# Transposing normalised rows by DMA instead of on TensorE, in two attention fronts

## The chip, the cores and the metric

One core of a Trainium2 chip runs the whole program. The metric is the time of one execution in device microseconds (us); lower is better. TensorE multiplies matrices (PE in the profile, PEld for its weight loads), VectorE is DVE, ScalarE is ACT, GpSimd is POOL, and SyncE (SP) issues nearly all DMAs, one after the other, from one queue.

## The reference

The input `A_x` has 2048 tokens of 512 features in bf16. Four layers are applied with residuals: attention, long convolution, attention, long convolution, each on layer-normalised rows.

```python
def _A_ref(x, wqkv, wo):             # H = 32 heads of Dh = 16, W = 8 keys, dilation 2
    qkv = (x @ wqkv).reshape(B, S, 3, H, Dh).transpose(2, 0, 3, 1, 4)
    q, k, v = qkv[0], qkv[1], qkv[2]
    idx = pos[:, None] - 2 * arange(8)[None, :]; mask = idx >= 0
    kg, vg = k[:, :, idx], v[:, :, idx]          # idx clipped at 0
    logits = einsum("bhsd,bhswd->bhsw", q, kg) * Dh ** -0.5
    attn = softmax(where(mask, logits, -1e9), axis=-1)
    return einsum("bhsw,bhswd->bhsd", attn, vg) -> (B, S, D) @ wo
def _B_ref(u, A, B, C, log_dt, Dskip):
    K = real(einsum("dn,dnl,dn->dl", C, exp(dt * A * l), dt * B))   # 2048 taps per feature
    return irfft(rfft(u) * rfft(K)) [first 2048] + u * Dskip
x = x + _A_ref(layernorm(x), A_wqkv, A_wo)
x = x + _B_ref(layernorm(x), ...)
x = x + _A_ref(layernorm(x), A_wqkv, A_wo)
x = x + _B_ref(layernorm(x), ...)
```

## The kernel before

**Tokens.** Token 16p + a lies on partition p in slot a (a = 0..15). A block b is four slots, that is 512 tokens; there are four blocks. `x_blk` and `xn` hold the normalised rows of one block, 128 partitions x (4 slots x 512 features).

**A front** is what each attention layer does before its core: normalise the rows of a block, turn them so that features lie on the partitions (`xnT`), and multiply by the weights. For block b, `front_t(b)` makes 16 TensorE transposes of 128x128 (L205) into two PSUM tiles `pt` and copies these out (L208). `front_k(b)` makes the keys: 4 feature tiles ft, each of 4 accumulating matmuls of 512 columns (L219), whose result is cast into `kT_ext` (L222). `front_q` and `qproj1` do the same for queries (L162, L164). `front_ext` copies keys shifted by one partition into the 14 slots ahead of block 0 in `kT_ext`, by four DMAs (L230) or on VectorE (L232).

**First front.** It runs inside `k_gen`, which makes the 2048 filter taps. `tables(c)` are VectorE products (L1076 to L1090) for chunk c of four, in two buffers (`A_t`). `products(c)` are 128 TensorE matmuls (L1111) that read them, and ScalarE casts their results into `kgs` (L1115). After chunks 1 and 3, 24 small DMAs store `kgs` to DRAM (`kd_dram`, L1129). The order of the work is written out by hand: each engine, SP among them, does its instructions in the order of the program text (`manual_schedule`), so front(b) stands between products(b-1) and products(b), except that front(3) and the queries of block 1 stand ahead of products(3). Row statistics (L81, L86) and normalising (L136) are ScalarE's for blocks 0 to 2; both are VectorE's for block 3 (L79, L138). `x_load(2)` and `x_load(3)` refill the buffers of blocks 0 and 1. After front(3) come `front_ext(3)`, the products of queries and keys (`mult`, L273) and their sums on TensorE (`lsum`, L280); `mx` (L338) takes the maximum of the sums on VectorE.

**Second front.** It follows the first convolution layer, whose last steps are `i2(1, t)` for t = 0..3 (L806 to L808): the inverse transform of half the features of block t, added to the residual `x_sb` by VectorE (L811) or ScalarE (L814). For block b, VectorE takes statistics (`stats` L91, `aggr` L1301), ScalarE computes the reciprocal deviation (`power`, L96 and L97), VectorE normalises (`norm`, L126 and L138). The loop as it stands:

```python
        for b in range(3):
            if b == 0:
                aggr(1); power(1); norm(1)
            keys(b, 0, 1, 2)
            pt = la.front_t(b + 1, ("act", "dve"), True)
            pt[0]()
            if b < 2:
                stats(b + 2)
            pt[1]()
            keys(b, 3)
            if b < 2:
                aggr(b + 2); power(b + 2); norm(b + 2)
```

The keys of block 3 and the queries of block 0 follow within the attention core (`last`). `warm` (L185) issues matmuls whose results nobody reads. `load_wv` and `load_wo` (L238, L245) load the weights of values and output; the filter spectra for the last layer are loaded into `kf_ring` (L744, L746).

**Memory.** The buffer of `xnT` is used again: as `u`, the input of the convolution, and as `z0`, an intermediate of its inverse transform.

Of the kernel before, what the change touches and what calls it, by code (L numbers as in the profile page):

```python
# [13 lines left out]
PSUM = bass.MemoryType.PSUM  # L14
F32 = mybir.dt.float32
BF16 = mybir.dt.bfloat16
# [4 lines left out]
P = 128  # L21
S = 2048
D = 512
# [3 lines left out]
NA = 16  # L27
NDT = 4
# [112 lines left out]
class LayerA:  # L141
# [16 lines left out]
    def qproj1(self, q, ft, qT, ps, tag):  # L158
        nc = self.nc
        pq = ps.tile([P, 512], F32, name="pq", tag=tag)  # L160
        for dt in range(NDT):
            nc.tensor.matmul(pq[:], lhsT=self.wqk[:, dt, ft * P:(ft + 1) * P],  # L162
                             rhs=self.xnT[:, dt, q * 512:(q + 1) * 512], start=(dt == 0), stop=(dt == NDT - 1))
        nc.scalar.copy(qT[:, ft].rearrange("p a q -> p (a q)"), pq[:])  # L164

    def q_tile(self, q):
# [6 lines left out]
    def front_open(self):  # L173
        tc = self.tc
        self.fctx = ExitStack()
        l = self.layer
        self.fp = self.fctx.enter_context(tc.tile_pool(name=f"a{l}_front", bufs=2, side="right"))
        self.ps_tr = self.fctx.enter_context(tc.tile_pool(name=f"a{l}_ps_tr", bufs=2, space=PSUM, side="right"))
        self.ps_pj = self.fctx.enter_context(tc.tile_pool(name=f"a{l}_ps_pj", bufs=2, space=PSUM, side="right"))
        self.pj_tag = "pp"  # L180
        self.nc.gpsimd.memset(self.kT[:, :, 0:14, 0:1], 0.0)
# [14 lines left out]
        for a in range(4):  # L196
            ln_apply(self.nc, self.xn[:, a, :], x_rows[:, a, :], rn[0], rn[1], a, ln_eng[a])

    def front_t(self, b, ev_eng, defer=False):
        nc, xn, evs = self.nc, self.xns.pop(b), []  # L200
        for dp in range(2):
            pt = self.ps_tr.tile([P, 2, 4, P], BF16, name="pt")
            for di in range(2):
                for a in range(4):
                    nc.tensor.transpose(pt[:, di, a, :], xn[:, a, (2 * dp + di) * P:(2 * dp + di + 1) * P], self.c["ident"][:])  # L205
            dst = self.xnT[:, 2 * dp:2 * dp + 2, b * 512:(b + 1) * 512]
            f = nc.scalar.copy if ev_eng[dp] == "act" else nc.vector.tensor_copy
            evs.append(lambda f=f, dst=dst, pt=pt: f(dst, pt[:].rearrange("p t a q -> p t (a q)")))  # L208
        if not defer:
            for f in evs:  # L210
                f()
        return evs

    def front_k(self, b, ev_eng, fts=range(NDT)):
        nc = self.nc
        for ft in fts:
            pp = self.ps_pj.tile([P, 512], F32, name="pp", tag=self.pj_tag)
            for dt in range(NDT):
                nc.tensor.matmul(pp[:], lhsT=self.wqk[:, dt, D + ft * P: D + (ft + 1) * P],  # L219
                                 rhs=self.xnT[:, dt, b * 512:(b + 1) * 512], start=(dt == 0), stop=(dt == NDT - 1))  # L220
            dst = self.kT[:, ft, 14 + b * 4: 18 + b * 4, :].rearrange("p a q -> p (a q)")
            (nc.scalar.copy if ev_eng[ft] == "act" else nc.vector.tensor_copy)(dst, pp[:])  # L222

# [61 lines left out]
    def core(self, x_sb, u, lnp, ev=None, nprod=0):  # L285

        tc, nc, lnst, l = self.tc, self.nc, self.lnst, self.layer
        ident, nident = self.c["ident"], self.c["nident"]
        scale = float(DH) ** -0.5
        xnT = self.xnT  # L290
# [9 lines left out]
        with ExitStack() as c2:  # L300
# [22 lines left out]
            def v_proj(a):  # L323
                pp = pq_tile()
                for dt in range(NDT):
                    nc.tensor.matmul(pp[:], lhsT=xnT[:, dt, a * P:(a + 1) * P],  # L326
                                     rhs=wv[:, dt, :], start=(dt == 0), stop=(dt == NDT - 1))
                nc.scalar.copy(v[:, 14 + a, :].rearrange("p (d h) -> p d h", h=H), pp[:].rearrange("p (h d) -> p d h", h=H))  # L328
                if a >= 14:
                    b = a - 14  # L330
                    nc.sync.dma_start(v[1:113, b:14:2, :], v[0:112, 16 + b:30:2, :])
                    nc.sync.dma_start(v[113:128, b:14:2, :], v[112:127, 16 + b:30:2, :])
                    event(("v", b))
# [131 lines left out]
            rows = [0, 2, 1, *range(3, NA)]  # L465
            for n in range(16):
# [13 lines left out]
                if n in (9, 10, 13, 14):  # L480
                    b0 = 0 if n < 11 else 4
                    r0 = b0 + (0 if n in (9, 13) else 2)
# [400 lines left out]
def k_gen(tc, nc, ident, ins, kd, la, x_v, lnst, b_consts, C):  # L883
# [4 lines left out]
    with ExitStack() as ctx:  # L888
# [7 lines left out]
        def x_load(b):  # L896
            xb[b] = la.fp.tile([P, 4, D], BF16, name="x_blk")
            nc.sync.dma_start(xb[b][:], x_v[:, b * 4:(b + 1) * 4, :])
# [8 lines left out]
        def ln_b(b):  # L907
            ln[b] = ln_end(nc, la.fp, ln[b])

        def apply(b, eng):  # L910
            la.front_apply(b, xb[b], ln[b], [eng] * 4, xb[b])

        def front(b):
            la.front_t(b, ["act"] * 2)
            if b == 0:
                x_load(2)
            la.front_k(b, ["act"] * 4)
            if b < 3:
                la.front_ext(b, "dma")

        with ExitStack() as ctx1:
# [41 lines left out]
            r = a_im  # L963
# [89 lines left out]
            ln_b(0)  # L1053
            run(1e9)
            apply(0, "act")
            front(0)
            stats(2, "act")
        tab = ctx.enter_context(tc.tile_pool(name="kg_tab", bufs=2))
# [71 lines left out]

        tables(0, {2: [lambda: ln_a(1, "act")], 3: [lambda: ln_b(1)]})
        apply(1, "act")
        x_load(3)
        products(0)
        la.front_q(0)
        front(1)
        tables(1, {2: [lambda: ln_a(2, "act")], 4: [lambda: ln_b(2)]})
        apply(2, "act")
        products(1)
        front(2)  # L1140
        C.update(next(bgen))
        tables(2, {3: [lambda: stats(3, "dve")], 4: [lambda: ln_a(3, "dve")]})
        products(2)
        tables(3, {1: [lambda: ln_b(3)], 2: [lambda: apply(3, "dve")]})
        front(3)
        la.front_q(1)
        la.front_close()
# [39 lines left out]
def kernel(  # L1187
# [31 lines left out]
               log_dt=B_log_dt, Dskip=B_Dskip)  # L1219
    x_v = A_x.rearrange("b (p a) d -> p (b a) d", p=P)  # L1220
    upool = ctx.enter_context(tc.tile_pool(name="xnT_u", bufs=1, side="right"))
    xnT = upool.tile([P, NDT, NA * P], BF16, name="xnT")
    u = xnT[:].rearrange("p t (b r) -> p (t b) r", r=64).rearrange("p q (a r) -> p q a r", r=4)
    la = LayerA(tc, nc, consts, lnst, A_wqkv, A_wo, 0, xnT, 2)

    C = {}
# [47 lines left out]
    krctx2.close()  # L1274
    la.close_logits()

    z0 = xnT[:].rearrange("p t c -> p (t c)").rearrange("p (m c) -> p m c", m=2 * NA)
    fb = FftB(tc, nc, C, consts["ident"], w2_dram, g2_dram, kf_dram, x_sb, 0)
    fb.z0, fb.ring_pool, fb.w2, fb.spare = z0, kpp, la.w2, la.spare()
    fb.ahead = 4  # L1280
# [8 lines left out]
    with tc.manual_schedule(engines=MAN):  # L1289
        fb.middle(lambda t: half_stats(nc, lnst, x_sb, t, 0), "act", "act")  # L1290
        fb.swap_psum()
        la.front_open()
        ln, agg = {}, {}

        def stats(b):
            half_stats(nc, lnst, x_sb, b, 1)

        def aggr(b):
            agg[b] = lnp.tile([P, 4, 2], F32, name="ln_ag")
            for a in range(4):  # L1300
                nc.vector.bn_aggr(agg[b][:, a, :], lnst["bn"][:, 4 * b + a, :, :])  # L1301

        def power(b):
            ln[b] = rstd_act(nc, lnp, agg[b][:, :, 1]), agg[b][:, :, 0], -1.0

        def norm(b):
            la.front_apply(b, x_sb[:, b * 4:(b + 1) * 4, :], ln_end(nc, lnp, ln[b]), ["dve"] * 4)

        def keys(b, *fts):
            la.front_k(b, ["act"] * 4, fts)  # L1310

        fb.i2(1, 0)
        fb.i2(1, 1, "act")
        stats(0)
        aggr(0)
        power(0)
        fb.i2(1, 2, "act")
        ev3 = fb.i2(1, 3, "act", True)
        norm(0)
        pt = la.front_t(0, ("act", "dve"), True)  # L1320
        stats(1)
        pt[0]()
        pt[1]()
        ev3()
        la.warm(la.ps_pj.tile([P, 512], F32, name="pp", tag=la.pj_tag), 4, la.wqk[:, 0, 0:512])
        for b in range(3):
            if b == 0:
                aggr(1)
                power(1)
                norm(1)  # L1330
            keys(b, 0, 1, 2)
            pt = la.front_t(b + 1, ("act", "dve"), True)
            pt[0]()
            if b < 2:
                stats(b + 2)
            pt[1]()
            keys(b, 3)
            if b < 2:
                aggr(b + 2)
                power(b + 2)  # L1340
                norm(b + 2)
            if b > 0:
                la.front_ext(b - 1, "dve")
        la.front_ext(2, "dve")
        la.front_close()
        fb.c_ps.close()
        fb.c_grp.close()
        krctx.close()

        def last(*fts):  # L1350
            for ft in fts:
                keys(3, ft)
                la.qproj1(0, ft, la.qT[0], la.ps_pj, la.pj_tag)

        ext = lambda ft: lambda: la.front_ext(3, "dve", ft)
        ev = {("m", 0, ft): [ext(ft)] for ft in range(NDT)}
        ev[("m", 0, 0)].insert(0, lambda: last(0, 1))
        ev[("q", 0, 0)] = [lambda: last(2)]
        ev[("q", 0, 1)] = [lambda: last(3)]
        ev[("p", 8)] = [lambda: la.load_w2(w2_dram)]  # L1360
        la.core(x_sb, u, lnp, ev)
# [60 lines left out]
```

## Time and profile before

| | |
|---|---|
| median of 3 runs | 455.67 us (454.72 to 457.34) |
| the profiled execution's own time | 455.0 us |
| its span | 453.2 us |
| PE matmul busy | 354.9 us, 78% |
| DVE busy | 402.2 us, 89% |
| ACT busy | 326.0 us, 72% |
| granted TensorE clock, mean | 0.98 |
| first front, from the first transpose to the last key matmul | 59.5 to 117.2 us |
| second front, the same | 285.2 to 308.1 us |

The profile is of one execution. All times in the text are counted from the start of its span; the time that the execution took in all is 1.8 us longer. An L with a number is a line of the kernel. In the chain of waits a row is start, duration, engine, tile and line, and the chain is what ended last, followed back. In a timeline a row is start, duration, engine, line, operation, output<-input and count, and at its end, in brackets, the idle time of the engine just before it and what ended that. SPq is SP issuing a DMA; its duration is the issue, not the transfer.

### The profile page before, as it was taken

The page shows a single profiled execution, that of the slowest core. Times are in us where ns is not written, and L with a number is a line of the kernel's source. Part 1 is how long each engine was busy: PE and PEld are TensorE (multiplying, and loading weights), DVE is VectorE, ACT ScalarE, POOL GpSimd, SP SyncE. Part 2 cuts the span into 40 slices and gives each one's busy share as a digit, 9 for nine tenths or more (in the row PEclk, how much of TensorE's full clock was granted, in tenths as well). Part 3 has the DMA queues.
Part 4 walks back from the last instruction along what each step waited for, and adds up shares of the span by engine and source line. Part 5 has one row for each costly group of instructions (what it writes and reads, how often), then busy time and mean ns, then how long its engine had stood idle before and what let it go on. Part 6 is the DMA issues. An engine that isn't in the chain of part 4 may idle for free.

```text
span 453.2 us, 12714 instructions
## 1 busy us (share of the span) xinstructions
PE 354.9 (78%) x5459; PEld 268.0 (59%) x5498; DVE 402.2 (89%) x558; ACT 326.0 (72%) x543; POOL 44.5 (10%) x46
## 2 busy tenths in 40 slices
PE   1000065888999989989898788999999899996885
PEld 1000034666676667767787787555657687776874
DVE  6799999999899999898897888889999999878964
ACT  5979979576555559967999886774654559699943
POOL 2000110100089300000400000000000020000000
PEclk9999997899999999999999999999999999998999
DMA  8920730121411575480266440670033053016714
GB/s 213 391 80 12 79 66 19 32 64 24 101 16 43 160 234 159 135 338 14 112 245 221 176 169 7 173 249 1 2 82 83 1 213 161 18 79 184 239 48 140
DMA packets 65354, 54.17 MB, mean 120 GB/s; under 512 B 36781, under 2 KB 53778, under 8 KB 64018
## 3 DMA queue, kind: packets, MB, share of 16 engines
q1 hardware_dynamic: 65154, 53.22, 38.8%
q8 instruction: 43, 0.70, 0.7%
q10 hardware_dynamic: 144, 0.13, 0.3%
q14 instruction: 13, 0.11, 0.1%
HBM read 30.28 MB, written 13.24 MB: 96 GB/s over the span
## 4 chain that ended last, share of the span: by engine, by line
PE 52%; ACT 20%; DVE 16%; DMA 7%; issue 3%; SPq 1%; DVEq 0%; ACTq 0%
PE po L385 9%; PE pp L219 6%; PE pq L326 6%; PE pq L162 5%; PE L L280 5%; PE pq L397 4%; PE pk L1111 4%; DVE t L757 4%; DVE pav L377 3%; ACT a1s L695 3%; DMA v_ext<-v_ext 3%; PE pb L713 2%; PE pb L706 2%; ACT ln_junk L86 2%; ACT ln_junk L81 2%
## 5 line engine op out<-in xcount | busy, mean ns | idle before, releaser
L377 DVE TENSOR_TENSOR pav<-attn,v_ext 128x4096 bf16<-128x4096 bf16 x32 | 72.7, 2282 | 0.5 <-DMA v_ext<-v_ext 0.5
L273 DVE TENSOR_TENSOR prod<-qT,kT_ext 128x4096 bf16<-128x4096 bf16 x29 | 66.2, 2299 | 1.1 <-ACT qT L164 0.6
L385 PEld LDWEIGHTS <-pav 128*128 128x128 bf16 x1024 | 58.6, 98 | 13.0 <-DVE pav L377 9.4
L385 PE MATMUL po<-ident,pav 128*128 128x128 bf16 x1024 | 62.5, 219 | 4.8 <-DVE pav L377 4.8
L205 PE MATMUL pt<-ident,x_blk 128*128 128x128 bf16 x64 | 5.6, 241 | 45.1 <-ACT x_blk L136 45.1
L791 PE MATMUL pb<-Wp,t 128*128 128x128 bf16 x256 | 31.0, 219 | 7.0 <-DVE t L757 4.6
L219 PE MATMUL pp<-xnT,kT_ext 128*128 128x512 bf16 x124 | 31.1, 393 | 4.0 <-ACT xnT L208 3.8
L776 ACT CAST ub<-pb 128x1024 bf16<-128x1024 f32 x32 | 32.0, 1039 | 2.5 <-DVE t L757 2.5
L119 POOL TENSOR_TENSOR ln_rstd<-ln_rstd,ln_mh 128x4 f32<-128x4 f32 x6 | 10.0, 1658 | 229.0 <-DVE ln_rstd L118 207.0
L1111 PE MATMUL pk<-B_t,A_t 128*64 128x84 bf16 (+1 forms) x512 | 27.0, 217 | 6.8 <-issue 3.5
L713 PE MATMUL pb<-a1s,w_sb 128*128 128x64 bf16 x768 | 31.0, 199 | 1.2 <-ACT ub L776 1.0
L328 ACT CAST v_ext<-pq 128x512 bf16<-128x512 f32 x32 | 18.7, 586 | 18.2 <-PE pq L326 18.0
L205 PEld LDWEIGHTS <-x_blk 128*128 128x128 bf16 x64 | 4.4, 108 | 46.3 <-ACT x_blk L136 46.0
L792 PE MATMUL pb<-WpJ,t 128*128 128x128 bf16 x256 | 30.6, 219 | 1.5 <-DVE t L757 1.5
L280 PEld LDWEIGHTS <-prod 128*128 128x128 bf16 x928 | 27.3, 96 | 7.4 <-DVE prod L273 1.5
L1111 PEld LDWEIGHTS <-A_t 128*64 128x64 bf16 (+1 forms) x512 | 24.7, 115 | 10.0 <-issue 5.9
L326 PE MATMUL pq<-wv,xnT 128*128 128x512 bf16 x119 | 30.3, 379 | 0.4
L162 PE MATMUL pq<-xnT,kT_ext 128*128 128x512 bf16 x121 | 30.0, 379 | 0.4 <-issue 0.2
L388 ACT CAST oT<-po 128x512 bf16<-128x512 f32 x32 | 18.5, 578 | 16.2 <-PE po L385 16.1
L397 PE MATMUL pq<-wop,oT 128*128 128x512 bf16 x110 | 29.3, 379 | 0.9
L713 PEld LDWEIGHTS <-w_sb 128*128 128x128 bf16 x768 | 27.5, 102 | 4.2 <-issue 1.6
L695 ACT CAST a1s<-pb 128x1024 bf16<-128x1024 f32 x28 | 27.4, 1027 | 2.4 <-PE pb L706 2.2
(221 smaller groups left out, 883.9 us busy)
## 6 DMA issues: line engine op xcount, KB each, us to landing
w_sb<-w_dram SPq DMA_DIRECT2D x8, 1024.0 KB
w_dram<-w_zero SPq DMA_DIRECT2D x1, 4096.0 KB
kf_ring<-kf_dram SPq DMA_DIRECT2D x16, 256.0 KB
kf_ring<-kf_dram SPq DMA_DIRECT2D x32, 128.0 KB
v_ext<-v_ext SPq DMA_DIRECT2D x4, 784.0 KB
x_blk<-in_A_x_dram SPq DMA_DIRECT2D x4, 512.0 KB
kT_ext<-in_A_wqkv_dram SPq DMA_DIRECT2D x4, 512.0 KB
x_sb<-in_A_x_dram SPq DMA_DIRECT2D x4, 512.0 KB
```

Of the source, the lines that this page charges most:

```text
L162: nc.tensor.matmul(pq[:], lhsT=self.wqk[:, dt, ft * P:(ft + 1) * P], rhs=self.xnT[:, dt, q * 512:(q + 1) * 512], start=(dt == 0), stop=(dt ...
L219: nc.tensor.matmul(pp[:], lhsT=self.wqk[:, dt, D + ft * P: D + (ft + 1) * P], rhs=self.xnT[:, dt, b * 512:(b + 1) * 512], start=(dt == 0), ...
L273: nc.vector.tensor_tensor(pr, self.qT[q][:, ft].unsqueeze(1).to_broadcast([P, W, 4, P]), kap, ALU.mult)
L280: self.nc.tensor.matmul(L[:, al, w, ft * 8:(ft + 1) * 8], lhsT=pr[:, w, al, :], rhs=self.c["ind8"][:], start=(ft == 0 and w == 0 and al % ...
L326: nc.tensor.matmul(pp[:], lhsT=xnT[:, dt, a * P:(a + 1) * P], rhs=wv[:, dt, :], start=(dt == 0), stop=(dt == NDT - 1))
L377: nc.vector.tensor_tensor(pv[:], attn[:, n % 4].unsqueeze(2).to_broadcast([P, W, DH, H]), vap, ALU.mult)
L385: nc.tensor.matmul(po[:, ft, :], lhsT=pvf[:, w, ft * P:(ft + 1) * P], rhs=ident[:], start=(w == 0 and ft == 0), stop=(w == W - 1), skip_gr ...
L397: nc.tensor.matmul(pw[:], lhsT=oT[:, ftp, :], rhs=wo[:, ftp, :], start=False, stop=(ftp == NDT - 1))
L695: (nc.scalar.copy if eng == "act" else nc.vector.tensor_copy)(dst, src)
L713: nc.tensor.matmul(p2[:, j, :], lhsT=self.w2[:, ec * EC + j, :], rhs=a1s[:, ec * EC + j, :], start=True, stop=True)
L776: nc.scalar.copy(ub[:], p2)
L1111: nc.tensor.matmul(o, lhsT=lhs, rhs=Bt[:, ri, c * CH + ql].rearrange("p b g -> p (b g)"), start=(not half and j % 4 == 0 and ri == 0), sto ...
```

## The change

`front_t` no longer uses TensorE. One DMA per block, issued from SP, reads the normalised rows (128 x 2048) and writes them transposed. `xnT` is laid out by slot, [slot][feature tile][token], so that a block is one piece of 2048 elements per partition, and each transposed 128x128 square lies together. The key and query matmuls read their 512 columns as four runs of 128. The PSUM pool for the transposes is gone.

In the first front the DMA is issued right after the rows are normalised, and so ahead of products(b-1) for blocks 1 and 2, and within tables(3) for block 3. In the second front the statistics, the normalising and the DMA of block b+2 are issued between the keys of block b, so that up to two blocks are under way; `i2(1, 2)` and `i2(1, 3)` stand behind norm(0) and norm(1), and 8 warming matmuls take the place of 4.

```diff
-            nc.tensor.matmul(pq[:], lhsT=self.wqk[:, dt, ft * P:(ft + 1) * P],
-                             rhs=self.xnT[:, dt, q * 512:(q + 1) * 512], ...)
+            nc.tensor.matmul(pq[:].rearrange("p (a q) -> p a q", q=P), lhsT=self.wqk[:, dt, ft * P:(ft + 1) * P],
+                             rhs=self.xnT[:, 4 * q:4 * q + 4, dt, :], ...)
...
-    def front_t(self, b, ev_eng, defer=False):
...
+    def front_t(self, b, rows=(0, 4)):
+        r0, r1 = rows
+        xn = self.xns[b]
+        self.nc.sync.dma_start_transpose(out=self.xnT[:, 4 * b + r0:4 * b + r1].rearrange("p a t q -> p (a t) q"),
+                                         in_=xn[:, r0:r1, :].rearrange("p a d -> p (a d)"))
...
             ln_b(0)
             run(1e9)
             apply(0, "act")
+            la.front_t(0)
             front(0)
...
         apply(1, "act")
+        la.front_t(1)
         x_load(3)
         products(0)
         la.front_q(0)
         front(1)
         tables(1, ...)
         apply(2, "act")
+        la.front_t(2)
         products(1)
         front(2)
...
-        tables(3, {1: [lambda: ln_b(3)], 2: [lambda: apply(3, "dve")]})
+        tables(3, {1: [lambda: ln_b(3)], 2: [lambda: apply(3, "dve"), lambda: la.front_t(3)]})
         front(3)
...
-    xnT = upool.tile([P, NDT, NA * P], BF16, name="xnT")
+    xnT = upool.tile([P, NA, NDT, P], BF16, name="xnT")
...
         power(0)
+        norm(0)
+        la.front_t(0)
         fb.i2(1, 2, "act")
-        ev3 = fb.i2(1, 3, "act", True)
-        norm(0)
-        pt = la.front_t(0, ("act", "dve"), True)
         stats(1)
-        pt[0]()
-        pt[1]()
-        ev3()
-        la.warm(..., 4, la.wqk[:, 0, 0:512])
+        aggr(1)
+        power(1)
+        norm(1)
+        la.front_t(1)
+        fb.i2(1, 3, "act")
+        la.warm(..., 8, la.wqk[:, 0, 0:512])
         for b in range(3):
...
+            keys(b, 0, 1)
             if b < 2:
                 stats(b + 2)
                 aggr(b + 2)
                 power(b + 2)
                 norm(b + 2)
+                la.front_t(b + 2)
+            keys(b, 2, 3)
             if b > 0:
                 la.front_ext(b - 1, "dve")
```

More of the change, by code (lines that the diff above doesn't have):

```diff
@@ L161, in qproj1 @@
         for dt in range(NDT):
-            nc.tensor.matmul(pq[:], lhsT=self.wqk[:, dt, ft * P:(ft + 1) * P],
-                             rhs=self.xnT[:, dt, q * 512:(q + 1) * 512], start=(dt == 0), stop=(dt == NDT - 1))
+            nc.tensor.matmul(pq[:].rearrange("p (a q) -> p a q", q=P), lhsT=self.wqk[:, dt, ft * P:(ft + 1) * P],
+                             rhs=self.xnT[:, 4 * q:4 * q + 4, dt, :], start=(dt == 0), stop=(dt == NDT - 1))
         nc.scalar.copy(qT[:, ft].rearrange("p a q -> p (a q)"), pq[:])
@@ L177, in front_open @@
         self.fp = self.fctx.enter_context(tc.tile_pool(name=f"a{l}_front", bufs=2, side="right"))
-        self.ps_tr = self.fctx.enter_context(tc.tile_pool(name=f"a{l}_ps_tr", bufs=2, space=PSUM, side="right"))
         self.ps_pj = self.fctx.enter_context(tc.tile_pool(name=f"a{l}_ps_pj", bufs=2, space=PSUM, side="right"))
@@ L197, in front_apply @@
             ln_apply(self.nc, self.xn[:, a, :], x_rows[:, a, :], rn[0], rn[1], a, ln_eng[a])
-    def front_t(self, b, ev_eng, defer=False):
[L200 to L212, printed above, removed]
+    def front_t(self, b, rows=(0, 4)):
[3 more added lines that the diff above has]
+                                         in_=xn[:, r0:r1, :].rearrange("p a d -> p (a d)"))
     def front_k(self, b, ev_eng, fts=range(NDT)):
@@ L218, in front_k @@
             for dt in range(NDT):
-                nc.tensor.matmul(pp[:], lhsT=self.wqk[:, dt, D + ft * P: D + (ft + 1) * P],
-                                 rhs=self.xnT[:, dt, b * 512:(b + 1) * 512], start=(dt == 0), stop=(dt == NDT - 1))
+                nc.tensor.matmul(pp[:].rearrange("p (a q) -> p a q", q=P), lhsT=self.wqk[:, dt, D + ft * P: D + (ft + 1) * P],
+                                 rhs=self.xnT[:, 4 * b:4 * b + 4, dt, :], start=(dt == 0), stop=(dt == NDT - 1))
             dst = self.kT[:, ft, 14 + b * 4: 18 + b * 4, :].rearrange("p a q -> p (a q)")
@@ L325, in v_proj @@
                 for dt in range(NDT):
-                    nc.tensor.matmul(pp[:], lhsT=xnT[:, dt, a * P:(a + 1) * P],
+                    nc.tensor.matmul(pp[:], lhsT=xnT[:, a, dt, :],
                                      rhs=wv[:, dt, :], start=(dt == 0), stop=(dt == NDT - 1))
@@ L913, in front @@
         def front(b):
-            la.front_t(b, ["act"] * 2)
             if b == 0:
@@ L1221 @@
     upool = ctx.enter_context(tc.tile_pool(name="xnT_u", bufs=1, side="right"))
-    xnT = upool.tile([P, NDT, NA * P], BF16, name="xnT")
-    u = xnT[:].rearrange("p t (b r) -> p (t b) r", r=64).rearrange("p q (a r) -> p q a r", r=4)
+    xnT = upool.tile([P, NA, NDT, P], BF16, name="xnT")
+    u = xnT[:].rearrange("p a t c -> p (a t c)").rearrange("p (q a r) -> p q a r", a=NA, r=4)
     la = LayerA(tc, nc, consts, lnst, A_wqkv, A_wo, 0, xnT, 2)
@@ L1275 @@
     la.close_logits()
-    z0 = xnT[:].rearrange("p t c -> p (t c)").rearrange("p (m c) -> p m c", m=2 * NA)
+    z0 = xnT[:].rearrange("p a t c -> p (a t c)").rearrange("p (m c) -> p m c", m=2 * NA)
     fb = FftB(tc, nc, C, consts["ident"], w2_dram, g2_dram, kf_dram, x_sb, 0)
@@ L1316 @@
         power(0)
+        norm(0)
+        la.front_t(0)
         fb.i2(1, 2, "act")
-        ev3 = fb.i2(1, 3, "act", True)
-        norm(0)
-        pt = la.front_t(0, ("act", "dve"), True)
         stats(1)
-        pt[0]()
-        pt[1]()
-        ev3()
-        la.warm(la.ps_pj.tile([P, 512], F32, name="pp", tag=la.pj_tag), 4, la.wqk[:, 0, 0:512])
-        for b in range(3):
[L1327 to L1333, printed above, removed]
+        aggr(1)
[3 more added lines that the diff above has]
+        fb.i2(1, 3, "act")
+        la.warm(la.ps_pj.tile([P, 512], F32, name="pp", tag=la.pj_tag), 8, la.wqk[:, 0, 0:512])
+        for b in range(3):
+            keys(b, 0, 1)
             if b < 2:
                 stats(b + 2)
-            pt[1]()
-            keys(b, 3)
-            if b < 2:
                 aggr(b + 2)
```

## The prediction

> **What bounds the kernel now.** I read the profile in four steps: busy shares, then the chain of waits in the two stretches that the change touches, then SP's own timeline, then the rows of what is removed. VectorE is busy 89% of the span, but an average over stages with different limits says nothing about these stretches. The chain of waits does (start us, us, engine, tile, line):
>
> ```profile
> 78.66 5.03 PE pk L1111 x64
> ...
> 87.90 1.84 ACT xnT L208 x2
> ...
> 93.58 2.83 ACT x_blk L136 x4
> ...
> 100.72 1.84 ACT xnT L208 x2
> ...
> 112.15 1.84 ACT xnT L208 x2
> 113.99 0.04 issue
> 114.03 3.18 PE pp L219 x14
> 117.22 3.45 PE pq L162 x16
> 120.67 5.61 PE pk L1111 x128
> 126.28 1.69 PE L L280 x64
> ```
>
> The reader is to see that in the first front ScalarE and TensorE hand the chain to each other, that the copies of the transposes (L208) are on it, and that from 114.03 on nothing but TensorE stands on it: keys of block 3, queries (L162), the last products (L1111), the first logit sums (L280). Who delays keys(3) delays everything behind it. The second front has the same form:
>
> ```profile
> 284.75 1.39 DVE xn L138 x4
> 286.19 0.90 PE pt L205 x13
> ...
> 290.71 0.89 PE pt L205 x16
> ...
> 295.06 0.95 PE pt L205 x16
> ...
> 299.46 0.95 PE pt L205 x16
> 300.41 1.73 PE pp L219 x8
> ```
>
> Here 0.9 us of TensorE transposes stands before the keys of each block, on the chain. SP, which will issue the new DMAs, shows in its timeline:
>
> ```profile
> 100.75 15.69 SPq L1129 DMA_DIRECT2D kd_dram<-kgs  x24
> 116.55 2.74 SPq L230 DMA_DIRECT2D kT_ext<-kT_ext  x4
> 119.46 0.53 SPq L238 DMA_DIRECT2D wv<-in_A_wqkv_dram  x1
> ...
> 285.19 0.37 SPq L238 DMA_DIRECT2D wv<-in_A_wqkv_dram  x1
> ```
>
> SP needs 15.69 us for 24 small stores, 0.65 us each, and starts nothing else meanwhile.
>
> [...] So a DMA whose input is ready still stands behind what is ahead of it on SP. The trace agrees: the four kT_ext copies of block 2 (L230) start at 116.55, though their casts (L222) ended at 106.41. [...] the PEclk row of the profile page does not show it: after the long idle time before 59.5 us the first 9 key matmuls took 3.68 us (409 ns each), while 14 of block 3 took 3.18 us (227 ns each). 16 keys then cost 5.2 us, not 3.5.
>
> **The price of one transpose.** T(b), 128x2048 bf16 = 512 KB from SBUF to SBUF, is in no row of before. Call L its time from issue to landing. From below: a plain copy. The first 127 KB copy of L230, issued at 116.55, lets VectorE start L273 at 119.14, so 2.6 us; the other 385 KB at the 213 to 391 GB/s that the page's busy slices show add 1.0 to 1.8, so about 4. [...] I take **L = 6**, as plain packets stand ahead in the same queue[...]. A gain below 4 has no reason, since a plain copy costs that.
>
> **Front 1, step by step (L = 6).** Removed: 64 TensorE transposes (16 per block, 1.07 us warm) and 8 ScalarE copies of 1.02 us; of these the chain holds three pairs of 1.84. Added: four T on SP. The matmuls read 4 runs of 128 instead of 512 in a row; I cost that at nothing, as L345 reads in several dimensions too and takes its 0.29 us per matmul; if it weren't so, the 379 ns of L219 would show it.
> - T(0): normalising (L136) ends at 61.61, T(0) lands at 67.6; before, keys started at 63.47. Cold in both, they end at 72.8 instead of 68.7: +4.1. Queued behind their casts on ScalarE: statistics of block 2, apply(1), and kgs copies that release products(0). Those end at 87.9 instead of 83.7; VectorE wants that buffer at 87.48, so it loses 0.4 only. Block 2's load waits for T(0) too, and comes in time.
> - T(1) starts at 82.2 and lands at 88.2; TensorE comes to keys(1) only at 91.5. Hidden behind products(0) and queries; without that cover it would cost its L. Of the 4.1 us late, 1.84 copies and a stall come back: keys(1) end at 95.0 against 93.0, +2.0.
> - The same +2.0 passes through apply(2), products(1), kgs: ready at 102.7 (before 100.73). T(2), ahead of the stores on SP, is issued at 98.4[...]; it lands at 104.4, keys(2) run to 107.9, products(2) to 113.5.
> - T(3) is where it decides. In the built order SP has: T(2), 24 kd stores, 4 copies of kT_ext, T(3), wv. Its input is ready near 108.5 (L138 at 107.11, 1.38 us), but the stores run 102.7 to 118.4, the copies to 121.3. T(3) starts at 121.4 and lands at 127.4. TensorE has been idle for 14 us, so cold: keys(3) end at 132.6 against 117.22, **+15.4**. Behind them in TensorE's order stand L162, L1111 and L280, 10.8 us without slack, then L338 on VectorE, which already waits 0.21 us for them. VectorE itself idles from 117 to about 130 (ext(3), L232, needs the casts). [...]
>
> **Front 2 (L = 6).** Removed: 64 transposes, of which 0.90 + 0.89 + 0.95 + 0.95 = 3.7 us are on the chain, 4 copies each on ScalarE (1.02) and VectorE (0.67), mostly beside other work. Added: T(0) to T(3), 4 more warming matmuls (0.9 us in idle time), and waits. On SP a kf_ring load now stands ahead of T(0); it waits for the last matmul of i2(1,3), as wv did at 285.19, and its issue takes up to 1.55 us (L744 at 288.89). So T(0) starts at 286.8, not before norm(0)'s end at 286.1, and lands at 292.8; the warming ends at 286.6, so keys(0) run cold: the first two ft end at 296.2 (8 x 0.43), all at 298.0. Before, they started at 287.8. "Two blocks ahead" holds for T(1) (norm(1) ends at 290, SP free at 291.5, lands at 297.5). But power(2) stands on ScalarE behind keys(0)'s two casts: 297.1, + 2.2 for rstd, nb and norm: T(2) 299.3, lands 305.3. Keys(1) run 298.0 to 301.5; casts, power(3), norm(3): 302.9, SP free at 303.3, T(3) lands at 309.3, after keys(2) (305.3 to 308.8). keys(3) start at 309.3 against 301.3: **+8.0**. From there on layer 1 is unchanged and follows.
>
> Sum: 15.4 + 8.0 = 23.4 us on the profiled execution's 455.0 (span 453.2, 1.8 around it; the median of the runs is 455.67, 0.15% above): **478.4, I say 478**. At L = 4 the same steps give 11.4 + 3.5, so 470; at L = 10, 24 + 17, so 496. Each us of L counts about four times: twice in front 1 (T(0) shifts the stores, then T(3)), twice in front 2 (T(0), then T(2) and T(3)).
>
> **Rivals.**
> - *The transpose itself is the bound* [...]
> - *Short DMA* (L near 3). The T(3) queue stays: 118.5 + 3, cold: +9.5, front 2 +1; 466. Against: a plain copy is no faster than 4.
> - *Faster: T(3) is not held on SP.* If the stores went out as quickly as the DMA engines take them (the page has them only 0.1 to 0.5 busy there) and L were 2.5, T(3) would land by 112.1; front 1 would keep the three pairs, 5.5, less 1 for T(0), front 2 about 1: 450. It decides from a landing of T(3) before 114. Against: SP's 0.65 us per store is its own issue time, and the order is in the program.
> - *The two-block lead is not what runs*, as T(0) stands behind i2(1,3): counted above, since norm(0) ends only 0.7 us earlier.
>
> **How the numbers follow.** Likeliest, L from 4 to 8: 0.72 (470 to 487, with 478 at my L). L from 8 to 13: 0.10 (up to 505). [...] Short: 0.05, 464 to 470. Faster rival: 0.03; no change, if slack behind front 1 took up the delay: 0.01. The range 464 to 506 leaves out the long transposes and the rivals that are not slower, 0.13 or so. Slower by over 0.5% (about what a measurement can tell from no change) 0.96, within 0.01, faster 0.03.
>
> **What would show it.** In the profile after: T rows on SP; T(3) issued near 121 directly after L220's copies (L230 now) and TensorE idle before keys(3) by 10 us or more, named as a DMA wait; the first key matmuls behind it at about 430 ns; VectorE idle in the same place; in front 2 TensorE idle before keys(0), keys(2) and keys(3). I am wrong if T(3) lands before 114, if L is under 3 or over 13, or if L219's matmuls get slower when warm.

## The result and the profile after

The changed kernel takes **474.06 us** (median of 4 runs, 470.73 to 474.42) against 455.20 us for the kernel before on the same chip (4 runs); the ratio is 1.039, 95% interval 1.033 to 1.045. It is slower, by some 18.9 us. The forecast was 478.0, with a range from 464 to 506. The profiled execution took 474.42 us, with a span of 472.6; the one before took 455.0, with 453.2.

Lines have moved: in the profile after, L201 is the DMA transpose T(b), L209 the key matmuls (L219 before), L212 their casts (L222), L220 the kT_ext copies (L230), L1119 the kd stores (L1129), L1101 the products (L1111), L263 `mult` (L273), L270 `lsum` (L280). SP's own timeline in the first front:

```profile
61.82 1.45 SPq L201 DMA_TRANSPOSE xnT<-x_blk  x1
...
82.12 1.72 SPq L201 DMA_TRANSPOSE xnT<-x_blk  x1
...
97.45 1.81 SPq L201 DMA_TRANSPOSE xnT<-x_blk  x1
101.77 15.40 SPq L1119 DMA_DIRECT2D kd_dram<-kgs  x24
117.28 2.74 SPq L220 DMA_DIRECT2D kT_ext<-kT_ext  x4
120.12 1.51 SPq L201 DMA_TRANSPOSE xnT<-x_blk  x1
```

T(0), T(1) and T(2) are issued when their rows are ready. T(3) is issued at 120.12, straight behind 24 stores and 4 copies. The chain of waits names the same place; it runs for 18 us along SP's single stores and copies, and then:

```profile
119.42 0.60 SPq L220
...
120.12 4.38 DMA xnT<-x_blk
124.50 0.04 issue
124.54 6.38 PE pp L209 x16
130.92 3.45 PE pq L162 x16
134.38 5.61 PE pk L1101 x128
139.99 2.49 PE L L270 x96
```

Before, keys(3) ended at 117.22 and queries, products and sums followed without a gap. They follow without a gap again, but from 130.92 on: +13.7 us. TensorE's timeline shows the wait, and what the clock makes of it. The two rows are the keys of block 2 and of block 3, with the same 16 matmuls:

```profile
101.77 3.61 PE L209 MATMUL pp<-xnT,kT_ext 128*128 128x512 bf16 x16 [0.78 <-DMA xnT<-x_blk]
...
124.54 6.38 PE L209 MATMUL pp<-xnT,kT_ext 128*128 128x512 bf16 x16 [13.56 <-DMA xnT<-x_blk]
```

The row of the granted clock on the profile page shows it too, in its 10th and 11th slice (106 to 130 us after), where the kernel before had nines; the mean is 0.952, and was 0.980. Before and after:

```profile
PEclk9999997899999999999999999999999999998999
PEclk9999998897599999999999899799999899998989
```

Taken finer, the recorded clock falls to one half at 113.1, 2.1 us after TensorE came to rest, and rises again at 130.2, 5.6 us after keys(3) began. Until 130.04 the weight loads of keys(3) follow each other every 0.43 us; the 16 queries of before, 3.62 us, are 0.22 us each. "Cold" and "warm" mean these two paces.

The chain in the second front holds both of the exposed transfers, T(0) and T(3), and between them the casts of ScalarE that delay the deviation of block 3 (L97):

```profile
297.04 4.92 DMA xnT<-xn
...
302.00 8.14 PE pp L209 x24
...
310.16 0.59 ACT kT_ext L212
...
310.88 0.21 ACT ln_rstd L97
...
311.32 1.38 DVE xn L138 x4
...
312.73 4.32 DMA xnT<-xn
...
317.09 1.02 PE pp L209 x4
```

Before, keys(3) of this front started at 301.27, the middle of the eight matmuls from 300.41 in the chain before. VectorE's residual adds ahead of the front are 10.8 us late (L811 at 270.29 before, L801 at 281.10 after), so of the 15.8 us by which keys(3) are late the front itself adds 5.0.

### The profile page after: what moved, and what is told of

It is laid out like the page before. It is cut to its first block, busy times and chain, and to the rows that moved or that the text cites. A ratio compares the mean times of both kernels' runs of the same rounds, so it can differ in the third digit from the quotient of the medians.

```text
span 472.6 us, 12473 instructions
## 1 busy us (share of the span) xinstructions
PE 353.4 (75%) x5345; PEld 262.5 (56%) x5374; DVE 399.9 (85%) x554; ACT 315.0 (67%) x531; POOL 44.5 (9%) x46
## 4 chain that ended last, share of the span: by engine, by line
PE 49%; ACT 18%; DVE 13%; DMA 11%; SPq 5%; issue 3%; DVEq 0%; ACTq 0%
PE po L375 8%; PE pp L209 6%; PE pq L316 6%; PE pq L162 5%; PE pq L387 5%; PE L L270 4%; DVE t L747 3%; SPq L1119 3%; ACT a1s L685 3%; PE pk L1101 3%; PE pb L696 2%; PE pb L703 2%; ACT ln_junk L86 2%; DMA xnT<-xn 2%; DVE pav L367 2%
## 5 line engine op out<-in xcount | busy, mean ns | idle before, releaser
L209 PE MATMUL pp<-xnT,kT_ext 128*128 128x512 bf16 x128 | 37.7, 458 | 70.7 <-DMA xnT<-x_blk 64.7
L367 DVE TENSOR_TENSOR pav<-attn,v_ext 128x4096 bf16<-128x4096 bf16 x32 | 72.8, 2283 | 1.5 <-DMA v_ext<-v_ext 1.1
L263 DVE TENSOR_TENSOR prod<-qT,kT_ext 128x4096 bf16<-128x4096 bf16 x29 | 66.6, 2314 | 6.0 <-PE pk L1101 5.0
L209 PEld LDWEIGHTS <-kT_ext 128*128 128x128 bf16 x128 | 14.3, 113 | 92.2 <-issue 82.1
L212 ACT CAST kT_ext<-pp 128x512 bf16<-128x512 f32 x32 | 18.8, 586 | 41.9 <-PE pp L209 41.9
L781 PE MATMUL pb<-Wp,t 128*128 128x128 bf16 x256 | 32.4, 224 | 6.5 <-DVE t L747 4.9
L782 PE MATMUL pb<-WpJ,t 128*128 128x128 bf16 x256 | 32.0, 224 | 1.5 <-DVE t L747 1.5
L270 PEld LDWEIGHTS <-prod 128*128 128x128 bf16 x928 | 27.3, 96 | 7.4 <-DVE prod L263 1.5
L1101 PE MATMUL pk<-B_t,A_t 128*64 128x84 bf16 (+1 forms) x512 | 24.6, 207 | 8.5 <-ACT kgs L1105 7.5
L378 ACT CAST oT<-po 128x512 bf16<-128x512 f32 x32 | 18.6, 581 | 16.2 <-PE po L375 16.0
L781 PEld LDWEIGHTS <-t 128*128 128x128 bf16 x256 | 25.7, 100 | 5.9 <-DVE t L747 5.9
L1101 PEld LDWEIGHTS <-A_t 128*64 128x64 bf16 (+1 forms) x512 | 22.6, 108 | 11.3 <-issue 7.4
```

The costliest lines, as they stand in the source:

```text
L209: nc.tensor.matmul(pp[:].rearrange("p (a q) -> p a q", q=P), lhsT=self.wqk[:, dt, D + ft * P: D + (ft + 1) * P], rhs=self.xnT[:, 4 * b:4 * ...
L263: nc.vector.tensor_tensor(pr, self.qT[q][:, ft].unsqueeze(1).to_broadcast([P, W, 4, P]), kap, ALU.mult)
L270: self.nc.tensor.matmul(L[:, al, w, ft * 8:(ft + 1) * 8], lhsT=pr[:, w, al, :], rhs=self.c["ind8"][:], start=(ft == 0 and w == 0 and al % ...
L367: nc.vector.tensor_tensor(pv[:], attn[:, n % 4].unsqueeze(2).to_broadcast([P, W, DH, H]), vap, ALU.mult)
L781: nc.tensor.matmul(p3[:, j, :], lhsT=t1[:, dql, :], rhs=wp_r, start=True, stop=False)
L782: nc.tensor.matmul(p3[:, j, :], lhsT=t2[:, dql, :], rhs=wpj_r, start=False, stop=True)
```

## The experiments

Each kernel is the changed one with the edit named. Times are medians, ratios against the kernel before on the same chip. Where a trace is compared, it is by four places in VectorE's timeline, in us later than in the profiled execution before: the first maximum of layer 0 (131.85 before), the residual add ahead of the second front (281.07), the first maximum of layer 1 (316.17) and the last residual add (447.31). The third less the second is what the second front costs. Such a place in one execution is good to a few us only: the layout alone stands 2 to 6 us early in its trace, and has the median of before. The clock is part of that: the second 64 matmuls of products(0) took 5.03 us in the profiled execution before, at a recorded clock of 0.50, and 2.91 in two of the kernels below that have the same work ahead of them (mixed, and hidden ones only).

Line numbers move from kernel to kernel, so go by the tiles of a row: pp<-xnT,kT_ext are keys, pq<-xnT,kT_ext queries, pk<-B_t,A_t the products, kd_dram<-kgs the stores, A_pr<-qT,kT_ext the first `mult`.

| kernel | median us | ratio, 95% interval | 1st max | add | max, layer 1 | last add |
|---|---|---|---|---|---|---|
| changed | 474.06 | 1.039, 1.033 to 1.045 | +13.7 | +10.8 | +16.0 | +19.8 |
| layout alone | 453.86 | 0.998, 0.996 to 1.001 | -2.0 | -5.7 | -5.7 | -4.2 |
| second front alone | 458.78 | 1.008, 1.005 to 1.011 | -2.1 | -4.4 | -0.3 | +4.5 |
| first front alone | 469.92 | 1.034, 1.028 to 1.040 | +14.5 | +12.3 | +12.3 | +13.4 |
| 16 stores behind T(3) | 462.47 | 1.018, 1.013 to 1.022 | +5.8 | +3.9 | +8.5 | +7.3 |
| keys(3) warmed | 468.95 | 1.032, 1.027 to 1.036 | +10.5 | +11.1 | +16.2 | +14.7 |
| deviation early | 470.06 | 1.035, 1.031 to 1.040 | +13.9 | +12.1 | +14.9 | +16.3 |
| all DMA, reordered | 455.82 | 1.005, 1.002 to 1.007 | -2.1 | -0.9 | +1.0 | +3.1 |
| mixed | 453.83 | 1.000, 0.998 to 1.003 | -1.1 | -3.9 | -3.9 | -3.8 |
| hidden ones only | 450.92 | 0.995, 0.992 to 0.997 | -2.4 | -4.9 | -4.9 | -3.7 |

**The layout alone.** Both fronts on TensorE again, in the order of before, but into the layout by slot; key and query matmuls read four runs of 128.

```diff
-            la.front_t(0) ... la.front_t(3)         # DMA
+            la.front_tp(b, ["act"] * 2)             # 16 TensorE transposes, 2 copies into xnT[:, 4b:4b+4, 2dp:2dp+2, :]
```

> Both fronts on TensorE transposes in their old order; only the layout by token slot is left, so keys and queries read four runs of 128. Theory: costs nothing, 455 within 1.5 us, and 379 ns per key matmul. Rival: four runs are read slower, 5% on the 252 key and query matmuls of 217 ns is 2.7 us, 20% is 11.

Measured: 453.86 us over 20 runs. The layout costs nothing that shows: the mean of the 128 key matmuls is 386 ns here (page, L226), 393 before.

**One front alone.** The second front by DMA and the first as in the experiment above, and the other way round.

> First front on TensorE transposes again (in the slot layout), second front as changed. Theory: only the second front's loss is left, 5.2 us at its end by the two traces, and perhaps the 3 to 4 us by which the shift grew behind it: 460 to 464. Rival (the two fronts are not separate, the second loses only because the first made it late): within 2 us of 455.

> First front as changed, second front with TensorE transposes and in its old order (in the slot layout). Theory: 13.7 us at the end of the first front, of which 2.9 come back in waits of layer 0: 466, between 464 and 469. If e2 and e3 add up to the whole (19 us), the fronts are separate. Rival (most of the loss lies in the second front and behind it): under 462.

Measured: 458.78 and 469.92, one just below its expected range, the other just above; so 4.4 and 15.6 us over the kernel before (454.35 in those runs), 20.0 together; the whole change costs 18.9. The fronts add up, within what the intervals allow, and the first has most of it. Traces agree: +14.5 at the first maximum for one, 4.1 in the second front for the other.

**Sixteen of the 24 stores behind T(3).** Only SP's order changes.

```diff
-                        nc.sync.dma_start(dst, sr)
+                        if c == 1 and n >= 8: held.append((dst, sr))     # the last 16
+                        else: nc.sync.dma_start(dst, sr)
...
         la.load_wv(...)
+        for dst, sr in held: nc.sync.dma_start(dst, sr)
```

> The changed kernel, with the last 16 of the 24 kd stores of chunk 1 issued on SP behind T(3) and the wv load instead of ahead of them. Theory (SP's order holds T(3)): T(3) starts right behind the four kT_ext copies, near 109.5, and lands near 114; [...]keys(3) run warm, and end near 117.5 instead of 130.9. The whole is 10.8 to 13.4 us faster than the changed kernel: about 461 to 463. Rival (what costs is the transfer or its contention with the stores, not its place): T(3) lands about as late or takes 8 us or more, and the time stays within 4 us of 474. Second rival (the stores are needed early): the gain is given back where the filter is read (k_rl loads), and VectorE waits there.

Measured: ratio 1.018 instead of 1.039, some 10 us back, from the order of sixteen small DMAs. SP's timeline in that kernel:

```profile
102.45 5.46 SPq L1124 DMA_DIRECT2D kd_dram<-kgs  x8
108.02 3.19 SPq L220 DMA_DIRECT2D kT_ext<-kT_ext  x4
111.31 3.31 SPq L201 DMA_TRANSPOSE xnT<-x_blk  x1
```

and its TensorE:

```profile
116.61 6.37 PE L209 MATMUL pp<-xnT,kT_ext 128*128 128x512 bf16 x16 [4.94 <-DMA xnT<-x_blk]
```

T(3) lands at 116.6, 8 us earlier than in the changed kernel, but still 5 us after TensorE is free, and the clock is cold all the same: 6.37 us. It is later than I had thought: the four copies ahead of it take 3.2 us of SP, and its own transfer 5.25. So the median lies in the expected range in part by luck: at the first maximum the trace wins 7.9 us, where the theory had keys(3) end 13.4 earlier. The first rival, that the transfer and not its place is what costs, falls all the same.

**Keys(3) warmed.** 60 matmuls whose results nobody reads, between products(2) and keys(3), where TensorE stands idle.

```diff
         tables(3, ...)
+        la.warm(la.ps_pj.tile([P, 512], F32, name="pp", tag=la.pj_tag), 60, la.wqk[:, 0, 0:512])
         front(3)
```

> The changed kernel with 60 warming matmuls on TensorE between products(2) and keys(3) of the first front, where it stands idle for 13.6 us; nothing else moves. Theory (2.9 us of the first front's 13.7 are the cold clock after that idle time): the 16 key matmuls of block 3 take about 3.5 us instead of 6.4, 471 to 472. Rival (what stands behind keys(3) is not bound by it[...]): 474 or more.

Measured: 468.95, a little below the expected range. The intervals of this and of the changed kernel overlap, so it is the trace that tells. T(3) lands 0.5 us earlier only (124.0); what differs is the clock:

```profile
110.08 12.90 PE L184 MATMUL pp<-kT_ext,ident 128*128 128x512 bf16 x58 [0.16 <-issue]
124.07 3.61 PE L209 MATMUL pp<-xnT,kT_ext 128*128 128x512 bf16 x16 [1.09 <-DMA xnT<-x_blk]
```

3.61 us instead of 6.38: 2.8 of the first front's 13.7 are the cold clock. The mean granted clock is 0.978 here, and 0.952 in the changed kernel.

**The deviation early, in the second front.** One line moves.

```diff
         for b in range(3):
-            keys(b, 0, 1)
             if b < 2:
                 stats(b + 2); aggr(b + 2); power(b + 2); norm(b + 2); la.front_t(b + 2)
+            keys(b, 0, 1)
             keys(b, 2, 3)
```

> The changed kernel with one thing moved in the second front: statistics, deviation, normalising and T of block b+2 are issued ahead of keys(b, 0, 1) instead of behind them. Theory (the second front loses because power(2) and power(3) stand behind key casts on ScalarE, and so T(2) and T(3) start late): power no longer waits 4.3 us, T(3) lands about 4 us earlier, and the second front costs 1 to 3 us instead of 5.2: 470 to 472. Rival (T(0) and its cold keys are the whole cost, keys(3) would then be late anyway): 474.

Measured: 470.06. The intervals of this and of the changed kernel overlap, so the times alone don't tell it; the traces do. VectorE's waits for the deviation of block 2, in the changed kernel and in this one:

```profile
306.56 0.16 DVE L126 SCALAR_TENSOR_TENSOR ln_nb<-ln_ag,ln_rstd 128x4 f32<-128x4 f32 x1 [4.26 <-ACT ln_rstd L97]
```

```profile
304.07 0.16 DVE L126 SCALAR_TENSOR_TENSOR ln_nb<-ln_ag,ln_rstd 128x4 f32<-128x4 f32 x1 [0.51 <-ACT ln_rstd L97]
```

and this kernel's TensorE then does the keys of blocks 0 to 2 and the first four matmuls of block 3 in one stretch:

```profile
303.20 13.87 PE L209 MATMUL pp<-xnT,kT_ext 128*128 128x512 bf16 x52 [4.29 <-DMA xnT<-xn]
```

The front costs 2.9 us instead of 5.2. What is left should be T(0), for which TensorE still waits 4.29 us, and the cold start behind it (13.87 us for 52 matmuls, where 16 warm ones take 3.6); that was not tried by itself.

**All transposes by DMA, only orders changed.** All 24 stores and block 2's copies stand behind T(3), block 3 is normalised one step earlier in tables(3), and the deviation is early as above.

```diff
-        tables(3, {1: [ln_b(3)], 2: [apply(3), front_t(3)]})
+        tables(3, {1: [ln_b(3), apply(3), front_t(3), front_ext(2, "dma")]})
```

> All eight transposes stay DMAs; only orders differ from the changed kernel: all 24 kd stores of chunk 1 and block 2's kT_ext copies behind T(3) on SP, block 3 normalised one step earlier, and in the second front the deviation of block b+2 ahead of the keys of block b. Theory (the loss is one of order: T(3) behind the stores, power behind the casts; what stays is T(0) of each front, which nothing covers): front 1 gives 12 to 15 us back, front 2 2 to 4: 455 to 460. Rival (the transposes themselves cost, by traffic or by time on SP): no better than the version with 16 stores behind T(3), 462 or more.

Measured: 455.82, ratio 1.005. The same eight transposes, and 3.4 of the 3.9% are gone. TensorE:

```profile
111.00 3.61 PE L209 MATMUL pp<-xnT,kT_ext 128*128 128x512 bf16 x16 [0.87 <-DMA xnT<-x_blk]
114.45 3.62 PE L162 MATMUL pq<-xnT,kT_ext 128*128 128x512 bf16 x16
```

The queries start at 114.45, 2.6 us ahead of the profiled execution before (117.05) and level with that of the layout alone (114.47). It is given back later. VectorE in layer 0, at the first product with the values (`v_ext`, which is filled up by copies as `kT_ext` is):

```profile
156.63 2.29 DVE L367 TENSOR_TENSOR pav<-attn,v_ext 128x4096 bf16<-128x4096 bf16 x1 [3.93 <-DMA v_ext<-v_ext]
```

The stores now run on SP without a pause from 112.7 to 144.6, and the first two copies of v_ext (L321, L322) go out behind them, at 149.79 and 150.51, where they went at 147.59 and 148.30 before. VectorE comes to them 2 us earlier than before, and waits. That the stores make this wait is how the profile reads; it was not tried by itself.

**Mixed.** As above in the first front, but block 0 and the whole second front on TensorE.

> First front: block 0 and the whole second front go back to TensorE transposes; blocks 1 to 3 keep the DMA transpose, all 24 kd stores of chunk 1 and the four kT_ext copies of block 2 stand behind T(3) on SP, and block 3 is normalised one step earlier in tables(3). Theory (a DMA transpose costs nothing where its 4.4 us lie beside other work and SP is free): T(3) lands by about 112, before TensorE has done products(2), so keys(3) find no wait and no cold clock; three pairs of transposes and copies leave the chain, part of the 5.5 us: 449 to 451, 3 to 5 us under the time before. Rival (whatever the order, transposes by DMA disturb the first front by their traffic and the pairs are not on the path): 454 to 458.

Measured: 453.83, the same as before, and 3 us above the expected range. The transfer did what the theory said (4.25 us, landed at 110.8). The cover was gone: products(2) are done at 107.3, 2.8 us earlier than in the reordered kernel. Block 0, back on TensorE, is one reason, and the pace of the matmuls another: the second 64 of products(0) took 2.91 us here and 5.03 there.

```profile
110.85 5.30 PE L226 MATMUL pp<-xnT,kT_ext 128*128 128x512 bf16 x16 [3.52 <-DMA xnT<-x_blk]
```

**The hidden ones only.** So only T(1) and T(2) of the first front stay DMAs; blocks 0 and 3 and the second front are on TensorE; the stores stand where they stood.

```diff
         def front(b):
+            if b in (0, 3):
+                la.front_tp(b, ["act"] * 2)
...
-        tables(3, {1: [ln_b(3)], 2: [apply(3), front_t(3)]})
+        tables(3, {1: [ln_b(3), apply(3)]})
```

> DMA transposes only for blocks 1 and 2 of the first front, the two whose 4.4 us lay wholly beside other work; blocks 0 and 3 and the second front on TensorE; the stores stay where they were before. Block 3 is normalised one step earlier in tables(3). Theory (a hidden transpose takes its pair of TensorE transposes and ScalarE copies, 1.84 us, off the chain): two pairs less, keys(3) warm and ending about 113, 3 to 4 us earlier than before; VectorE's tables(3), which end near 116, then bound products(3), so 450 to 452.5, ratio 0.990 to 0.997. Rival (VectorE is the bound there already, or the pairs were not on the chain): no difference, ratio 0.998 to 1.003.

Measured: **450.92 us**, ratio 0.9947, interval 0.9922 to 0.9972, over 22 runs. That is about half a per cent less than the kernel before, and the shortest time of all. TensorE and VectorE at the end of this front:

```profile
107.03 1.07 PE L206 MATMUL pt<-ident,x_blk 128*128 128x128 bf16 x16
...
112.75 3.62 PE L162 MATMUL pq<-xnT,kT_ext 128*128 128x512 bf16 x16
116.21 5.77 PE L1119 MATMUL pk<-B_t,A_t 128*128 128x84 bf16 x128
```

```profile
116.14 0.68 DVE L1093 TENSOR_TENSOR A_t<-A_t,pow_t 128x1024 bf16<-128x1024 bf16 x1
116.74 0.28 DVE L239 COPY kT_ext<-kT_ext 128x508 bf16<-128x508 bf16 x1
117.11 2.29 DVE L280 TENSOR_TENSOR A_pr<-qT,kT_ext 128x4096 bf16<-128x4096 bf16 x1
```

The queries start at 112.75 instead of 117.05, and L280 follows the tables at once. Before, VectorE waited there:

```profile
119.14 2.29 DVE L273 TENSOR_TENSOR A_pr<-qT,kT_ext 128x4096 bf16<-128x4096 bf16 x1 [1.99 <-PE pq L162]
```

The row names the queries of block 1, but this `mult` takes those of block 0, and in the changed kernel it starts ahead of them (127.45 and 130.76). What fits is the first copy of block 2 on SP, issued at 116.55 before and at 112.18 here.

Where the half per cent comes from, these traces do not show. The layout alone, with every transpose on TensorE, has its queries at 114.47 in an execution that was as short (450.76 us), and the same `mult` is no later there than here:

```profile
117.06 2.29 DVE L280 TENSOR_TENSOR A_pr<-qT,kT_ext 128x4096 bf16<-128x4096 bf16 x1
```

So the 1.7 us by which TensorE is ahead of it do not reach VectorE, whose tables run to 116.7 in both, and the first maxima lie 0.4 us apart. Nor is T(2) wholly hidden: TensorE waits 0.79 us for it. The medians differ all the same (ratios 0.998 and 0.995); whether that is the hidden transposes or the earlier normalising of block 3 was not tried and stays open.

## Why the prediction was right, and where it was off

**The direction and the place held.** The prediction said that T(3) would be issued near 121 behind the stores and copies (120.12), that TensorE would be idle 10 us or more and then cold (13.56), and that the delay would pass undiminished through queries, products and sums (it does). The experiments show each part: with 16 stores fewer ahead T(3) lands 8 us earlier and the first maximum comes 7.9 us earlier; a warm clock gives 2.8 us; orders alone give nearly all of the loss back. The rival in which the transpose itself is the bound, whose size no trace had shown, fell with a transfer of 4.4 us; the faster one fell with SP's 0.64 us per store and T(3) landing at 124.5, not before 114.

**The mis-sized term is L.** I took 6 us from issue to landing, my estimate, where the rows of before gave about 4; T(0) and T(3) of the two fronts took 4.36, 4.38, 4.92 and 4.32 in the changed kernel, and T(3) took 4.25 to 5.25 in the experiments: 5.25 with sixteen stores behind it, where 12 DMAs had just gone out on SP, 4.25 in the mixed kernel, where none had for over 10 us. In the changed kernel SP is held 1.45 to 2.90 us by each; the times at which the prediction has SP free again rest on a longer hold, which no trace had shown. The lower bound, a plain copy, came closer: the profile page after has 4.0 us for the plain load of 512 KB that fills `x_blk` (KB, median us from issue to landing):

```profile
x_blk<-in_A_x_dram SPq DMA_DIRECT2D x4, 512.0 KB, 4.0
```

The transposes named here took 0.3 to 1.3 us more.

**First front: 15.4 predicted, 13.7 measured.** T(3) was issued 1.3 us earlier than I had it, and its transfer was 1.6 shorter. The earlier issue does not come from the shorter T(0): keys(0) took 6.5 us cold where I had 5.2, so they ended at 72.75, as I had it (72.8), and T(1) started at 82.12 (82.2). It comes from the second 64 matmuls of products(0), 4.2 us where I had kept the 5.0 of before, and from stores that took 15.4 us, not 15.7.

Against that, the 16 cold keys(3) took 6.4 us where I had 5.2. My 5.2 came from a row of before in which TensorE had been at transposes for some 4 us. From 0.43 us cold and 0.22 warm, an estimate for 6.4 us is 13 or 14 of 16 cold, 5.8 us, and the recorded clock has 5.6. How many are cold differs between executions: keys(0), behind 50.4 us of idle time in both, took 6.53 us in the changed kernel and 5.14 in the reordered one. That the recorded clock doesn't show the cold start held for keys(0) again, but not for keys(3), with slices of 7 and 5.

**Second front: 8.0 predicted, 5.0 measured at keys(3), 5.2 at the first maximum.** Less the 10.8 us by which the front is late, T(0) is issued at 286.2 (286.8 predicted) and lands at 291.2 (292.8); T(2) is issued at 297.4 (299.3), T(3) at 301.9 (303.3), landing at 306.3 (309.3). T(0) and T(3) together are 2.8 us shorter than my L. Behind 4.35 us of idle time keys(0) ran cold here too, as I had them: their weight loads lie 0.43 us apart from 302.38 to 307.50. The order that I wrote out, power(2) behind two casts, is what runs, and the experiment with the deviation early takes nearly half of the front's cost away. One wait that I named did not show in the changed kernel: T(2) landed as the casts of block 1 freed the buffer for keys(2) (idle 0.62 us, ended by ScalarE). With sixteen stores behind T(3) in the first front, where nothing differs in the second, it waits 1.08 us for it.

**The sum.** 13.7 and 5.2 make 18.9, which is also the difference of the medians. The profiled execution does not go straight there. After the first front it wins 2.9 us in layer 0, 1.7 of it at one wait of VectorE, in the handling of the filter, which lasted 2.36 us before and 0.63 after; in layer 1 it loses 3.8 again:

```profile
193.58 0.43 DVE L1256 COPY k_perm<-k_rl 128x1024 bf16<-128x1024 bf16 x1 [2.36 <-DMA g_dram<-k_perm]
```

```profile
205.50 0.43 DVE L1248 COPY k_perm<-k_rl 128x1024 bf16<-128x1024 bf16 x1 [0.63 <-ACT x_sb L393]
```

Neither is shown to belong to the change: in the kernel with keys(3) warmed, 10 us late like this one, that wait is 2.17 us and layer 1 wins 1.5. The granted clock differs between the two (0.952 and 0.978); whether it makes the difference in layer 1 stays open.

**An edit costed at nothing** was nothing: the matmuls in four runs take 3.61 us for 16 when warm, as 3.62 for the 16 queries of before.

## What to carry to other kernels

In these fronts a DMA that took work from busy engines cost what other work did not cover: in the first front of the changed kernel no wait for T(1), 0.78 us for T(2), 13.56 for T(3). Ask for each single one what TensorE does between issue and landing, and ask again after every other edit: in the mixed kernel products(2) were done 2.8 us earlier, and TensorE waited 3.52 us for T(3), not 0.87. Look at the issuing queue as at an engine: two dozen stores of 0.64 us that nobody waits for yet kept the one DMA behind them that somebody does wait for 11 us after its rows were ready (109.1). A wait of TensorE for a transpose could be paid twice, once idle and once in slower matmuls behind it: in the first front the 16 keys of block 3 took 5.30, 6.37 and 6.38 us behind waits of 3.52, 4.94 and 13.56 us, and 3.61 behind waits of 0.87 and 1.09. And moving the stores out of the way pays in full only if what they then stand in front of has the time; the later copies of `v_ext` in the reordered kernel suggest that it had not.

## What was not expected of the hardware

Transposing 512 KB of bf16 within SBUF by one DMA took 4.25 to 5.25 us, not much more than the plain load of 512 KB (4.0). It is finely cut, though. Packets, MB and share of the hardware queue before and after:

```profile
q1 hardware_dynamic: 65154, 53.22, 38.8%
q1 hardware_dynamic: 81794, 57.42, 42.2%
```

So there are 2,080 packets more for each of the eight transposes, of about 252 bytes each. The time for which SP is held by the issue is not a constant: 1.32 us for T(3) in the reordered kernel, where SP had issued nothing for 8 us, 3.31 in the one with sixteen stores behind it, where 12 DMAs had just gone out.

The recorded clock does not tell of every cold start. It stands at 1.00 all through keys(0) of the changed kernel, which took 6.53 us, and at one half through most of keys(3), which took 6.38.
